# Moving weight-chunk loads behind the last unit's routing in an attention, FFN and top-1 MoE kernel

## Chip, cores and metric

One core of one Trainium2 chip. The metric is device microseconds (us) of one execution of the whole kernel, the median of several runs.

## What is computed

Three stages, all fp32, on 4 x 576 = 2304 tokens of width 512: sliding-window attention, a gated FFN and a top-1 mixture of 8 experts.

```python
def _moe_ref(x, w1, w2, w3, w_out):          # x: attention output, 2304 x 512
    return ((x @ w1) * (x @ w2) @ w3) @ w_out

def _moe2_ref(x, w_gate, w_output_gate, w1, w2):
    e_idx = np.argmax(x @ w_gate, axis=1)
    gate_w = softmax(x @ w_gate)[np.arange(N), e_idx]
    eom = sigmoid(x @ w_output_gate)
    for e in range(8):
        mask = e_idx == e
        ye = np.maximum(x[mask] @ w1[e], 0) @ w2[e]      # 512 -> 1024 -> 512
        out[mask] = gate_w[mask, None] * eom[mask, e, None] * ye
```

## The kernel before

Every fp32 product is three TensorE passes (`PASSES`) over operands split into a high part and a low part in the fp32r format: ScalarE (ACT) writes the high part, VectorE (DVE) subtracts it from the source to get the low part. An expert's two weight matrices are 4 MB; they come as 8 chunks of 512 KB. `items` numbers them: items 0 to 3 are w1 of expert 0, 4 to 7 its w2, 8 to 11 w1 of expert 1, 12 to 15 its w2, and so on. `eload` (line 658) issues a chunk's load on SyncE's queue (SP; line 666 for w1, 668 for w2) into one of three buffers (`ck2`, and a fourth, `ck3`, later); `esplit` is the split: `ehigh` on ACT (line 680), `elow` on DVE (line 684), which frees the buffer, and then a call of `eload` for what may be loaded next.

Attention and FFN run in 9 units of 256 tokens. Up to the end of the last unit's FFN a planner (`Plan`, a list scheduler) sets the order; `plan_end` gives it the first 11 chunk loads and 8 splits. TensorE (PE) follows the order of the program text; on the other engines the framework orders what is independent, and each engine then works through its list strictly in order.

Routing of the last unit (units before it are routed already): `x2_turn` and `logit` compute the logits `lg`; `_first` and `_onehot` the best expert as a one-hot `oh` on DVE; `_sum` is three small PE matmuls `rps` (lines 356 to 360) that count tokens per expert; `_rank` turns them into row numbers `pos` (line 376), `_gate` into the weights `ent` and the counts; two `_scatter`s on GpSimd (POOL, line 389) write 8-byte rows (token, weight) to `tab` in DRAM, sorted by expert. The 11 pieces are the list `post`, taken one by one by `step`.

Meanwhile PE works on the static block of expert 0 (`static_block`), 256 rows of `tab` that earlier units filled: for each of 8 feature blocks f, 12 matmuls `hps` (line 927), whose result becomes the high and low part of relu on ACT and DVE (lines 932, 933); then for each of two row blocks 24 matmuls `yps` with w2 (line 908), item 4 + f/2 being needed from f on. `at1` says after which (f, kk) of the hps part something is called, `at2` and `at3` after which f of the two yps parts; `step`s and `esplit`s are placed there. `rest` reads the rest of the rows: `rows` loads index rows from `tab` (line 705) and issues the gathers of token rows on POOL (line 711).

After the static block come the row turns for expert 0's remaining rows and expert 1's (`xT_block`: 4 transposes `gps`, line 732, then the high part `exT` on ACT, line 421, and the low part on DVE, line 422; two PSUM banks, so the third turn waits until the first is read), then expert 0's row block (`row_block`, matmuls `rps` of line 961), and then the static blocks of experts 1 to 7 with a row block each where an expert has more than 256 rows.

Of the kernel before, what the change touches and what calls it, by code (L numbers as in the profile page):

```python
# [9 lines left out]
F32 = mybir.dt.float32  # L10
# [3 lines left out]
I32 = mybir.dt.int32  # L14
# [7 lines left out]
NT, DM, DF, NE = B * S, H * D, 1024, 8  # L22
# [3 lines left out]
NTILE = NT // 128  # L26
# [370 lines left out]
def attention_moe_moe_kernel(ctx: ExitStack, tc: tile.TileContext, q0, k0, v, w1, w2, w3, w_out,  # L397
                             w_gate, w_ogate, ew1, ew2, out):
    nc = tc.nc
# [8 lines left out]
    tab = dram.tile([NE * NT, 2], I32, name="tab")  # L408
# [24 lines left out]
    rt = Router(tc, const, ps_ab, "ab", tab)  # L433
# [196 lines left out]
    exp_state = {}  # L630
    ex = [None]
# [23 lines left out]
    items = [(e, i, c) for e in range(NE) for i in range(2) for c in range(4)]  # L655
    nload, nsplit = [0], [0]

    def eload(to):
        while nload[0] < min(to, len(items)):
            e, i, c = items[nload[0]]  # L660
            if ex[0] is not None and nload[0] % 4 == 3:
                t = ex[0].tile([128, 1024], F32, name="ck3", tag="ck3", bufs=1)
            else:
                t = exp_state["p"].tile([128, 1024], F32, name="ck2", tag="ck2", bufs=3)
            if i == 0:
                nc.sync.dma_start(out=t, in_=ew1[e, 128 * c:128 * c + 128, :])
            else:
                nc.sync.dma_start(out=t.rearrange("p (a d) -> p a d", a=2),
                                  in_=ew2[e, 256 * c:256 * c + 256, :].rearrange("(a p) d -> p a d", p=128))
            eq.append(t)  # L670
            nload[0] += 1
# [7 lines left out]
    def ehigh():  # L679
        nc.scalar.activation(out=eparts()[0], in_=eq[0], func=AF.Copy)  # L680

    def elow(low=V):
        hi, lo = eparts()
        low.tensor_tensor(lo, eq.popleft(), hi.bitcast(F32), op=ALU.subtract)  # L684
        nsplit[0] += 1

    def esplit(low=V):
        if nsplit[0] < len(items):
            ehigh()
            elow(low)  # L690
            eload(nsplit[0] + (3 if ex[0] is None else 4))

    def step(n=1):
        for _ in range(n):
            if post:
                f, *a = post.popleft()
                f(*a)

    idx, xg, xTs = {}, {}, {}

    def rows(e, src, blocks, queue=None):

        n = src.shape[0] // 128
        t = idx[e] = exp_state["p"].tile([128, 4, 2], I32, name="idx", tag="idx", bufs=NE)
        (queue or nc.sync).dma_start(out=t[:, 0:n, :], in_=src.rearrange("(j p) x -> p j x", p=128))
        for j in range(blocks):
            gather(e, j)

    def gather(e, j):
        g = xg[e, j] = exp_state["p"].tile([128, DM], F32, name="xg", tag="xg", bufs=6)  # L710
        nc.gpsimd.indirect_dma_start(out=g, out_offset=None, in_=x2d[:, :],  # L711
                                     in_offset=bass.IndirectOffsetOnAxis(ap=idx[e][:, j, 0:1], axis=0))

    def early_rows(part):

        if part == 0:
            rt.count(256)
            t = idx["early"] = exp_state["p"].tile([128, 2, 2], I32, name="ixe", tag="ixe")
            nc.sync.dma_start(out=t, in_=tab[0:256, :].rearrange("(j p) x -> p j x", p=128))
            g = xg["early"] = moe.tile([128, 4, DM], F32, name="xt1", tag="xt1")  # L720
            nc.vector.memset(g[:, 0:2, :], 0.0)
        else:
            j = part - 1
            top = UNIT * (NU - 1)
            nc.gpsimd.indirect_dma_start(out=xg["early"][:, j, :], out_offset=None, in_=x2d[0:top, :],
                                         in_offset=bass.IndirectOffsetOnAxis(ap=idx["early"][:, j, 0:1], axis=0),
                                         bounds_check=top - 1, oob_is_err=False)
# [15 lines left out]
    def early_high(j):  # L743
        nc.scalar.activation(out=xTs[0][:, 0, :, 128 * j:128 * j + 128], in_=tps["e", j], func=AF.Copy)
# [108 lines left out]
    def plan_end():  # L853

        o = P.add("SP", 0.0, 0, open_exp, [done["x", n] for n in range(B * NP)], lat=0)
        for j in range(11):
            done["el", j] = P.add("DMA", 1.4, 400 + 5 * j, lambda j=j: eload(j + 1), [o], take=[("ck2", ("ck2", j))], lat=2.0)
        for j in range(8):

            k, c = divmod(j, 4)  # L860
            old = [done["gate", NU - 1, 2 * c + 1, k - 1]] if k else []
            h = P.add("ACT", 1.06, 400 + 5 + 5 * j, ehigh, [done["el", j]] + old + ([done["es", j - 1]] if j else []))
            done["es", j] = P.add("DVE", 1.22, 400 + 5 + 5 * j, elow, [h], give=[("ck2", j)])
        r = done["rows", NU - 2]
        r = P.add("DVE", 0.5, 400, lambda: early_rows(0), [r, o, done["free", 10], done["free", 11]], lat=4.0)
        for j in (1, 2):
            x = P.add("POOL", 1.1, 400, lambda j=j: early_rows(j), [r], lat=3.0)
            x = P.add("PE", 0.46, 400 + 55, lambda j=j: early_turn(j - 1), [x], take=[("S", ("early", j))])
            x = P.add("ACT", 0.6, 400 + 55, lambda j=j: early_high(j - 1), [x])
            P.add("DVE", 0.65, 400 + 55, lambda j=j: early_low(j - 1), [x], give=[("early", j)])  # L870
# [46 lines left out]
    def static_block(e, ix, at1, at2, at3, h_tile=h_tile, y_tile=y_tile):  # L917

        w1e = eslot(e, 0)
        xT = xTs.pop(e)  # L920
        hT = []
        for f in range(8):
            ps = (ps_v if f % 4 == 3 else ps_ab).tile([128, 512], F32, name="hps", tag="pv" if f % 4 == 3 else "ab")
            for kk in range(4):
                c = 1024 * kk + 128 * f
                for i, (a, b) in enumerate(PASSES):
                    mm(ps[:, 0:256], lhsT=w1e[a][:, c:c + 128], rhs=xT[:, b, kk, :],  # L927
                       start=kk == 0 and i == 0, stop=kk == 3 and i == 2)
                if (f, kk) in at1:
                    at1[f, kk]()  # L930
            h = h_tile(f)
            nc.scalar.activation(out=h[:, 0, :], in_=ps[:, 0:256], func=AF.Relu)
            nc.vector.scalar_tensor_tensor(out=h[:, 1, :], in0=ps[:, 0:256], scalar=0.0,
                                           in1=h[:, 0, :].bitcast(F32), op0=ALU.max, op1=ALU.subtract)
            hT.append(h)
            if f in at1:
                at1[f]()
        w2e = eslot(e, 1)
        for j, at in enumerate((at2, at3)):
            ps = mm2(hT, 128 * j, w2e, at)  # L940
            emit_out(ps, ix, j, y_tile)
# [52 lines left out]
    def rest():  # L994

        n0 = nc.values_load(rt.done[0:1, 0:1], min_val=0, max_val=256)
        rows(0, tab[bass.ds(n0, 128), :], 1, nc.scalar)
        rows(1, tab[NT:NT + 512, :], 3, nc.scalar)

    at1 = {k: lambda n=n: step(n) for k, n in {(0, 2): 1, (1, 0): 1, (1, 2): 1, (2, 0): 3, (3, 2): 3, (4, 1): 2}.items()}  # L1000
    at1.update({f: esplit for f in (5, 6, 7)})
    static_block(0, idx["early"], at1, {0: rest, 1: esplit, 4: esplit, 7: esplit}, {2: esplit, 5: esplit}, h_first, y_first)
    s_mo2.close()
    s_mo1.close()
    s_moe.close()
# [19 lines left out]
    n0 = nc.values_load(rt.done[0:1, 0:1], min_val=0, max_val=256)  # L1025
    n = nc.values_load(rt.cnt[0:1, 0:1], min_val=0, max_val=NT)
# [2 lines left out]
    begin(1)  # L1029
    turn()  # L1030
    gather(1, 3)
    with tc.If(n > n0):
        row_block(xT, idx[0], 0, w1e, w2e)
        with tc.If(n > n0 + 128):  # L1034
            row_loop(n0 + 128, n, w1e, w2e, xT)
    for e in range(1, NE):
        at1 = {f: esplit for f in (0, 2, 4, 6)}
        at1[1] = turn
        at3 = {3: esplit, 6: esplit}
        if e + 1 < NE:  # L1040
            rows(e + 1, tab[e * NT + NT:e * NT + NT + 512, :], 4)
            at3.update({0: lambda e=e: begin(e + 1), 2: turn, 5: turn})
        static_block(e, idx[e], at1, {f: esplit for f in (1, 5)}, at3)
        w1e, w2e = eslot(e, 0), eslot(e, 1)
        n = nc.values_load(rt.cnt[0:1, e:e + 1], min_val=0, max_val=NT)  # L1045
        with tc.If(n > 256):  # L1046
            xT = xTs.pop((e, 2))
            row_block(xT, idx[e], 2, w1e, w2e)
            with tc.If(n > 384):  # L1049
                xT_block(xg[e, 3], xT, 0)  # L1050
                row_block(xT, idx[e], 3, w1e, w2e)
                with tc.If(n > 512):  # L1052
                    row_loop(e * NT + 512, e * NT + n, w1e, w2e, xT)
# [49 lines left out]
```

## Time and profile before

| what | us |
|---|---|
| median of three runs | 787.07 (786.39 to 788.73) |
| profiled execution | 785.67 |
| its span | 784.0 |
| PE busy in the span | 734.4 |
| mean granted clock of PE | 0.985 of full |

The profiled execution is 1.40 us under the median. All times below are us from the start of its span. The stretch that the change touches runs from the last unit's FFN (about 488) to the start of expert 1's block (543.46): some 56 us. A timeline row gives the start, the length, the engine, the line, the operation and its tiles, the number of instructions drawn together, and in brackets the idle time before it with what ended it. SPq and ACTq are the queues on which SP and ACT issue DMAs.

### The profile page before, as it was taken

What the parts mean: (1) busy time and instruction counts of PE and PEld (TensorE: products, weight loads), DVE (VectorE), ACT (ScalarE), POOL (GpSimd) and SP (SyncE); (2) the same over time, 40 slices, a digit from 0 to 9 for tenths busy, and PEclk for the clock granted to TensorE, in tenths of its full rate; (3) what the DMA queues carried; (4) which work ended last, traced back from release to release, by engine and by line L of the source; (5) the groups of instructions that cost most, each with busy time, mean ns of one, the idle gap of its engine ahead of it and who ended that gap; (6) DMA issues with size and microseconds to landing.
All of it is one profiled execution on the core that took longest, in us unless ns stands there. A gap on an engine that the chain in (4) does not pass through costs nothing. (4 is left out here: it accounts for less than half of the span.)

```text
span 784.0 us, 13573 instructions
## 1 busy us (share of the span) xinstructions
PE 734.4 (94%) x5227; PEld 658.0 (84%) x5227; DVE 377.2 (48%) x907; ACT 302.0 (39%) x683; POOL 168.1 (21%) x196
## 2 busy tenths in 40 slices
PE   3799989999999999999999999879999999999995
PEld 2577778999999999999999998767888998988874
DVE  6987995543544444444324233813534661661110
ACT  2554443433333243344222123524445563553221
POOL 6554553110111311110020001123112212111010
PEclk9999998999999999999999999999999999999998
DMA  8946762421322222005000001783726772750010
GB/s 326 408 167 217 213 210 84 152 79 31 111 91 87 78 77 77 31 28 189 28 1 28 1 28 48 244 174 109 247 88 233 258 246 90 251 156 28 5 41 14
DMA packets 38934, 97.47 MB, mean 124 GB/s; under 512 B 9748, under 2 KB 9876, under 8 KB 38849
## 3 DMA queue, kind: packets, MB, share of 16 engines
q1 hardware_dynamic: 33072, 83.06, 32.0%
q0 software_dynamic: 4816, 12.77, 5.0%
q8 instruction: 50, 0.82, 0.5%
q10 hardware_dynamic: 960, 0.53, 0.2%
q14 instruction: 36, 0.29, 0.1%
HBM read 86.83 MB, written 10.65 MB: 124 GB/s over the span
## 5 line engine op out<-in xcount | busy, mean ns | idle before, releaser
L560 PE MATMUL ab<-xt,w 128*128 128x256 f32 x1728 | 229.2, 287 | 0.1
L560 PEld LDWEIGHTS ab<-xt,w 128*128 128x128 f32 x1728 | 219.1, 193 | 4.8 <-DVE f L513 0.3
L584 PE MATMUL acc<-w,gt 128*128 128x512 f32 x432 | 114.4, 399 | 3.4 <-ACT gt L572 2.6
L584 PEld LDWEIGHTS acc<-w,gt 128*128 128x128 f32 x432 | 76.1, 189 | 17.4 <-ACT gt L572 3.1
L568 DVE TENSOR_TENSOR a_sb<-ab,a_sb 128x256 f32<-128x256 f32 x72 | 30.5, 423 | 121.9 <-PE ab L560 113.5
L908 PE MATMUL yps<-w,hT 128*128 128x512 f32 x336 | 82.3, 395 | 0.0
L177 POOL TENSOR_TENSOR pp<-pp,r 128x384 f32<-128x384 f32 x48 | 39.6, 828 | 191.7 <-DVE r L172 160.5
L908 PEld LDWEIGHTS yps<-w,hT 128*128 128x128 f32 x336 | 61.3, 188 | 11.6
L572 ACT ACTIVATE gt<-a_sb 128x256 fp32r<-128x256 f32 x72 | 30.0, 416 | 100.3 <-DVE a_sb L568 95.6
L684 DVE TENSOR_TENSOR w<-ck,w 128x1024 fp32r<-128x1024 f32 x48 | 58.1, 1220 | 21.0 <-ACT w L680 14.4
L540 PE MATMUL wps<-w,w3T 128*128 128x512 f32 x192 | 52.7, 417 | 11.7 <-ACT w3T L527 11.6
L680 ACT ACTIVATE w<-ck 128x1024 fp32r<-128x1024 f32 x48 | 50.3, 1057 | 27.0 <-DMA ck<-in_moe_w 24.4
L900 POOL DMA_INDIRECT out<-y,idx x20 | 20.1, 1003 | 178.5 <-ACT y L899 124.1
L163 ACT ACTIVATE pp<-sps,nm 128x128 f32<-128x128 f32 x144 | 42.3, 368 | 39.4 <-DVE nm L154 37.2
L540 PEld LDWEIGHTS wps<-w,w3T 128*128 128x128 f32 x192 | 35.5, 196 | 19.4 <-ACT w3T L527 11.6
L927 PEld LDWEIGHTS hps<-exT,w 128*128 128x128 f32 x384 | 46.4, 192 | 3.5 <-issue 2.2
L927 PE MATMUL hps<-exT,w 128*128 128x256 f32 x384 | 47.4, 284 | 1.9 <-PEq L1049 0.9
L565 ACT ACTIVATE a_sb<-ab 128x256 f32<-128x256 f32 x72 | 27.8, 386 | 55.1 <-PE ab L560 51.9
L389 POOL DMA_INDIRECT tab<-ent,pos x18 | 17.6, 980 | 139.5 <-DVE pos L376 42.2
L422 DVE TENSOR_TENSOR exT<-gps,exT 128x512 fp32r<-128x512 f32 x23 | 15.9, 691 | 58.9 <-ACT exT L421 58.9
L576 DVE TENSOR_TENSOR gt<-a_sb,gt 128x256 fp32r<-128x256 f32 x72 | 31.3, 434 | 25.4 <-ACT gt L572 24.4
L145 PE MATMUL sps<-k,q 128*128 128x128 f32 x288 | 41.4, 282 | 1.0 <-DMA k<-in_k 1.0
(132 smaller groups left out, 1025.6 us busy)
## 6 DMA issues: line engine op xcount, KB each, us to landing
ck<-in_moe_w SPq DMA_DIRECT2D x88, 512.0 KB
q<-in_q SPq DMA_DIRECT2D x16, 576.0 KB
v<-in_v SPq DMA_DIRECT2D x16, 576.0 KB
k<-in_k SPq DMA_DIRECT2D x16, 320.0 KB
w<-in_moe_w_out SPq DMA_DIRECT2D x8, 512.0 KB
w<-in_moe_w SPq DMA_DIRECT2D x8, 512.0 KB
x2d<-x SPq DMA_DIRECT2D x16, 256.0 KB
x2d<-x ACTq DMA_DIRECT2D x2, 256.0 KB
```

Source lines behind the costliest of these rows:

```text
L145: nc.tensor.matmul(ps[:, 128 * i:128 * i + 128], lhsT=s["q"][:, 128 * c:128 * c + 128], rhs=s["k"][:, 64 * c:64 * c + 128], start=False, s ...
L163: nc.scalar.activation(out=p[:, o], in_=ps[:, o], func=AF.Exp, bias=nm[:, i:i + 1], scale=0.125)
L177: nc.gpsimd.tensor_tensor(p, p, s.pop(("r", g)).unsqueeze(2).to_broadcast([128, 3, 128]), op=ALU.mult)
L540: mm(ps, lhsT=t[:, a, 128 * j:128 * j + 128], rhs=wo[b][:, o:o + 512], start=g == 0 and j == 0 and x == 0, stop=g == 1 and j == 3 and x == 2)
L560: mm(ps, lhsT=w[a][:, c:c + 128], rhs=x[:, b, kk, :], start=kk == 0 and i == 0, stop=kk == 3 and i == 2)
L568: V.tensor_tensor(asb[u, m], gps.pop((u, m, 1)), asb[u, m], op=ALU.mult)
L576: V.tensor_tensor(g[:, 1, :], asb.pop((u, m)), g[:, 0, :].bitcast(F32), op=ALU.subtract)
L584: mm(accs[u][t], lhsT=g[:, a, 128 * t:128 * t + 128], rhs=ws["w34"][b][:, 512 * m:512 * m + 512], start=m == 0 and i == 0, stop=m == 7 and ...
L680: nc.scalar.activation(out=eparts()[0], in_=eq[0], func=AF.Copy)
L684: low.tensor_tensor(lo, eq.popleft(), hi.bitcast(F32), op=ALU.subtract)
L908: mm(ps, lhsT=hT[f][:, a, c0:c0 + 128], rhs=w[b][:, 512 * f:512 * f + 512], start=f == 0 and i == 0, stop=f == 7 and i == 2)
L927: mm(ps[:, 0:256], lhsT=w1e[a][:, c:c + 128], rhs=xT[:, b, kk, :], start=kk == 0 and i == 0, stop=kk == 3 and i == 2)
```

## The change

A chunk load can now be held back: `eload(to, behind)` first lets POOL copy one column of `behind` into the chunk's tile, and the load, which overwrites that tile, waits for the copy. The planner issues 6 loads and 6 splits instead of 11 and 8. Items 6 and 7 (the second half of expert 0's w2) are loaded behind `pos` (function `second`, called at (4, 3)) and split at f = 7. `rest` moves from the first yps part to f = 5 of the hps part, loads index rows 0 and 1 on SP's queue (ACT's before), and then loads items 8 to 10 behind `idx[1]`. `_sum`, `_rank` and `_gate` move from (3, 2) to (4, 0), which is 6 hps matmuls later, the scatters from (4, 1) to (4, 2). Splits and loads of items 8 and up come later: two in the second yps part, two before the row block, 9 instead of 8 in each of the blocks of experts 1 to 4. There are 4 buffers for index rows instead of 8, so the index loads of experts 4 to 7 wait for a buffer.

```diff
--- before.py
+++ after.py
@@ -655,13 +655,16 @@
     items = [(e, i, c) for e in range(NE) for i in range(2) for c in range(4)]
     nload, nsplit = [0], [0]
 
-    def eload(to):
+    def eload(to, behind=None):
+
         while nload[0] < min(to, len(items)):
             e, i, c = items[nload[0]]
             if ex[0] is not None and nload[0] % 4 == 3:
                 t = ex[0].tile([128, 1024], F32, name="ck3", tag="ck3", bufs=1)
             else:
                 t = exp_state["p"].tile([128, 1024], F32, name="ck2", tag="ck2", bufs=3)
+            if behind is not None:
+                nc.gpsimd.tensor_copy(t[:, 0:1], behind.bitcast(F32))
             if i == 0:
                 nc.sync.dma_start(out=t, in_=ew1[e, 128 * c:128 * c + 128, :])
             else:
@@ -688,7 +691,8 @@
         if nsplit[0] < len(items):
             ehigh()
             elow(low)
-            eload(nsplit[0] + (3 if ex[0] is None else 4))
+            if nsplit[0] > 8:
+                eload(nsplit[0] + (3 if ex[0] is None else 4))
 
     def step(n=1):
         for _ in range(n):
@@ -701,7 +705,7 @@
     def rows(e, src, blocks, queue=None):
 
         n = src.shape[0] // 128
-        t = idx[e] = exp_state["p"].tile([128, 4, 2], I32, name="idx", tag="idx", bufs=NE)
+        t = idx[e] = exp_state["p"].tile([128, 4, 2], I32, name="idx", tag="idx", bufs=4)
         (queue or nc.sync).dma_start(out=t[:, 0:n, :], in_=src.rearrange("(j p) x -> p j x", p=128))
         for j in range(blocks):
             gather(e, j)
@@ -853,9 +857,9 @@
     def plan_end():
 
         o = P.add("SP", 0.0, 0, open_exp, [done["x", n] for n in range(B * NP)], lat=0)
-        for j in range(11):
+        for j in range(6):
             done["el", j] = P.add("DMA", 1.4, 400 + 5 * j, lambda j=j: eload(j + 1), [o], take=[("ck2", ("ck2", j))], lat=2.0)
-        for j in range(8):
+        for j in range(6):
 
             k, c = divmod(j, 4)
             old = [done["gate", NU - 1, 2 * c + 1, k - 1]] if k else []
@@ -994,12 +998,21 @@
     def rest():
 
         n0 = nc.values_load(rt.done[0:1, 0:1], min_val=0, max_val=256)
-        rows(0, tab[bass.ds(n0, 128), :], 1, nc.scalar)
-        rows(1, tab[NT:NT + 512, :], 3, nc.scalar)
-
-    at1 = {k: lambda n=n: step(n) for k, n in {(0, 2): 1, (1, 0): 1, (1, 2): 1, (2, 0): 3, (3, 2): 3, (4, 1): 2}.items()}
-    at1.update({f: esplit for f in (5, 6, 7)})
-    static_block(0, idx["early"], at1, {0: rest, 1: esplit, 4: esplit, 7: esplit}, {2: esplit, 5: esplit}, h_first, y_first)
+        rows(0, tab[bass.ds(n0, 128), :], 1)
+        rows(1, tab[NT:NT + 512, :], 3)
+        eload(11, idx[1][:, 0, 0:1])
+
+    at1 = {k: lambda n=n: step(n) for k, n in {(0, 2): 1, (1, 0): 1, (1, 2): 1, (2, 0): 3, (4, 0): 3, (4, 2): 2}.items()}
+
+    def second():
+        eload(8, rt.pos[:, NTILE - 1:NTILE])
+
+    def both():
+        esplit()
+        esplit()
+
+    at1.update({(4, 3): second, 5: rest, 7: both})
+    static_block(0, idx["early"], at1, {}, {4: esplit, 7: esplit}, h_first, y_first)
     s_mo2.close()
     s_mo1.close()
     s_moe.close()
@@ -1029,6 +1042,8 @@
     begin(1)
     turn()
     gather(1, 3)
+    for _ in range(2):
+        esplit()
     with tc.If(n > n0):
         row_block(xT, idx[0], 0, w1e, w2e)
         with tc.If(n > n0 + 128):
@@ -1040,7 +1055,7 @@
         if e + 1 < NE:
             rows(e + 1, tab[e * NT + NT:e * NT + NT + 512, :], 4)
             at3.update({0: lambda e=e: begin(e + 1), 2: turn, 5: turn})
-        static_block(e, idx[e], at1, {f: esplit for f in (1, 5)}, at3)
+        static_block(e, idx[e], at1, {f: esplit for f in ((1, 3, 5) if e < 5 else (1, 5))}, at3)
         w1e, w2e = eslot(e, 0), eslot(e, 1)
         n = nc.values_load(rt.cnt[0:1, e:e + 1], min_val=0, max_val=NT)
         with tc.If(n > 256):
```

DVE, from the last logits of the routing to the one-hot `oh`. Before:

```order
L617 COPY lg<-lps 128x16
L684 TENSOR_TENSOR w_5832<-ck_5639,w_5831 128x1024
L338 TENSOR_REDUCE mx<-lg 128x2
L933 SCALAR_TENSOR_TENSOR xt_5691<-hps,xt_5691 128x256
L339 TENSOR_TENSOR d<-lg,mx 128x16
L684 TENSOR_TENSOR w_5832<-ck_5835,w_5831 128x1024
L341 SCALAR_TENSOR_TENSOR w<-d,wt 128x16
L381 TENSOR_REDUCE se<-ex 128x2
L343 TENSOR_REDUCE wm<-w 128x2
L383 TENSOR_SCALAR se<-se 128x2
L348 TENSOR_TENSOR oh<-w,wm 128x16
```

Of the change:

```order
L617 COPY lg<-lps 128x16
L338 TENSOR_REDUCE mx<-lg 128x2
L339 TENSOR_TENSOR d<-lg,mx 128x16
L341 SCALAR_TENSOR_TENSOR w<-d,wt 128x16
L343 TENSOR_REDUCE wm<-w 128x2
L381 TENSOR_REDUCE se<-ex 128x2
L348 TENSOR_TENSOR oh<-w,wm 128x16
```

The two splits (tile `ck`, 128x1024) and the relu part between the steps of the one-hot are gone from there.

ACT, from the end of the hps part of expert 0's static block to the high part of expert 0's rows (`exT` with a number). Before:

```order
L932 ACTIVATE xt_5813<-hps 128x256 [waits PE_49] x2
L680 ACTIVATE w_5921<-ck_5925 128x1024 [waits DMAHW6_49]
L932 ACTIVATE xt_5813<-hps 128x256 [waits PE_49]
L996 TENSOR_LOAD done [waits DVE_49]
L705 ISA
L705 DMA idx<-tab 128x2 [waits DMAHW1_49,DMASW3_49]
L705 DMA idx<-tab 128x4x2
L899 ACTIVATE xg<-yps,ixe 128x512 [waits PE_49] x2
L421 ACTIVATE exT_6017<-gps 128x512 [waits DMASW1_49,DMASW0_49,DMAHW7_49,DVE_49,PE_49]
```

Of the change (`ck_5799` and `ck_5802` are items 6 and 7; `ck_5849`, `ck_5852`, `ck_5855` items 8 to 10; `xg<-yps` is the block's result):

```order
L936 ACTIVATE xt_5805<-hps 128x256 [waits PE_49] x4
L683 ACTIVATE w_5306<-ck_5799 128x1024 [waits DVE_49,DMAHW5_49,Pool_49]
L683 ACTIVATE w_5306<-ck_5802 128x1024 [waits DMAHW6_49,Pool_49]
L903 ACTIVATE xg<-yps,ixe 128x512 [waits DMAHW2_49,PE_49]
L683 ACTIVATE w_5938<-ck_5849 128x1024 [waits DMAHW3_49,Pool_49]
L683 ACTIVATE w_5938<-ck_5852 128x1024 [waits DMAHW4_49,Pool_49]
L903 ACTIVATE xg<-yps,ixe 128x512 [waits PE_49]
L683 ACTIVATE w_5938<-ck_5855 128x1024 [waits DMAHW5_49,Pool_49]
L421 ACTIVATE exT_5996<-gps 128x512 [waits DMASW1_49,DMASW0_49,DMAHW1_49,DVE_49,PE_49]
```

Expert 0's `exT` now stands behind the splits of items 6 to 10; DVE's list has the low parts in the same order.

POOL, from the last unit's scatters on. Before:

```order
L389 DMA tab<-ent,pos 18432x2 [waits DMASW2_49,DVE_49]
L389 DMA tab<-ent,pos 18432x2 [waits DMASW3_49]
L711 DMA xg<-x2d,idx 128x512 [waits DVE_49,DMAHW7_49,DMAHW1_49,DMASW4_49]
L711 DMA xg<-x2d,idx 128x512 [waits DMAHW2_49,DMASW5_49]
L711 DMA xg<-x2d,idx 128x512 [waits DMASW6_49]
L711 DMA xg<-x2d,idx 128x512 [waits DMASW7_49]
L900 DMA out<-xg,ixe 2304x512 [waits DMASW0_49,Activation_49]
```

Of the change:

```order
L389 DMA tab<-ent,pos 18432x2 [waits DMASW2_49,DVE_49]
L389 DMA tab<-ent,pos 18432x2 [waits DMASW3_49]
L667 COPY ck_5799<-pos 128x1 [waits Activation_49]
L667 COPY ck_5802<-pos 128x1 [waits Activation_49]
L715 DMA xg<-x2d,idx 128x512 [waits DVE_49,DMAHW4_49,DMAHW7_49,DMAHW3_49,DMASW4_49]
L715 DMA xg<-x2d,idx 128x512 [waits DMAHW0_49,DMASW5_49]
L715 DMA xg<-x2d,idx 128x512 [waits DMASW6_49]
L715 DMA xg<-x2d,idx 128x512 [waits DMASW7_49]
L667 COPY ck_5849<-idx 128x1 [waits Activation_49]
L667 COPY ck_5852<-idx 128x1 [waits DMAHW5_49,DVE_49]
L667 COPY ck_5855<-idx 128x1 [waits DMAHW6_49,DVE_49]
L904 DMA out<-xg,ixe 2304x512 [waits DMASW0_49,Activation_49]
```

The copies that hold items 6 and 7 stand behind the scatters, those of items 8 to 10 behind the four gathers of index rows 0 and 1.

## Rows read from the trace of the kernel before

**Rows 1.** The page's first part: busy time of the engines, share of the span, instructions.
```profile
PE 734.4 (94%) x5227; PEld 658.0 (84%) x5227; DVE 377.2 (48%) x907; ACT 302.0 (39%) x683; POOL 168.1 (21%) x196
```
**Rows 2.** Timeline of PE from the last FFN matmuls to the first yps.
```profile
490.10 1.68 PE L584 MATMUL acc<-w,gt 128*128 128x512 f32 x6 [1.65 <-ACT gt L572]
...
496.01 1.07 PE L614 MATMUL lps<-gates,xt 128*128 128x16 f32 x8 [0.42 <-DVE xt L933]
...
503.11 0.17 PE L356 MATMUL rps<-oh,tri 128*128 128x16 bf16 x1 [2.18 <-DVE oh L348]
...
503.53 7.86 PE L927 MATMUL hps<-xt,wx 128*128 128x256 f32 x51
511.23 11.07 PE L908 MATMUL yps<-w,xt 128*128 128x512 f32 x48
```
**Rows 3.** Timeline of DVE in the last unit's routing.
```profile
499.64 0.16 DVE L617 COPY lg<-lps 128x16 f32<-128x16 f32 x1
499.72 1.21 DVE L684 TENSOR_TENSOR w<-ck,w 128x1024 fp32r<-128x1024 f32 x1
...
501.35 1.22 DVE L684 TENSOR_TENSOR w<-ck,w 128x1024 fp32r<-128x1024 f32 x1
...
502.89 0.17 DVE L348 TENSOR_TENSOR oh<-w,wm 128x16 bf16<-128x16 f32 x1
...
505.41 0.17 DVE L376 CAST pos<-pf 128x2 int32<-128x2 f32 x1
```
**Rows 4.** Windows: stretch, length, busy of five engines, then PEclk, DMA share, GB/s.
```profile
504.00:508.00 4.00, 4.00 (x24) 4.00 (x23) 2.91 (x11) 2.77 (x4) 1.77 (x2) 0.57 0.81 260
508.00:512.00 4.00, 4.00 (x33) 3.87 (x32) 3.15 (x5) 2.10 (x4) 0.21 (x1) 1.00 0.74 43
```
**Rows 5.** Timeline of SP's queue and ACT: two chunk loads, each with its first use.
```profile
487.02 0.38 SPq L668 DMA_DIRECT2D ck<-in_moe_w  x1
490.65 1.06 ACT L680 ACTIVATE w<-ck 128x1024 fp32r<-128x1024 f32 x1 [0.60 <-DMA ck<-in_moe_w]
493.00 0.33 SPq L666 DMA_DIRECT2D ck<-in_moe_w  x1
497.94 1.06 ACT L680 ACTIVATE w<-ck 128x1024 fp32r<-128x1024 f32 x1 [2.14 <-DMA ck<-in_moe_w]
```
**Rows 6.** Timeline, the group of tokens before: second scatter, index load, first gather.
```profile
467.79 0.96 POOL L389 DMA_INDIRECT tab<-ent,pos  x1 [0.30 <-issue]
471.03 0.39 SPq L719 DMA_DIRECT2D ixe<-tab  x1
476.12 1.04 POOL L725 DMA_INDIRECT xt<-x2d,ixe  x1 [7.38 <-issue]
```
**Rows 7.** Timeline, the last unit: second scatter, a chunk load, index load, two gathers.
```profile
507.25 0.96 POOL L389 DMA_INDIRECT tab<-ent,pos  x1 [0.30 <-issue]
508.68 0.34 SPq L666 DMA_DIRECT2D ck<-in_moe_w  x1
513.96 1.03 ACTq L705 DMA_DIRECT2D idx<-tab  x2
520.71 0.98 POOL L711 DMA_INDIRECT xg<-x2d,idx  x1 [12.50 <-issue]
522.55 0.96 POOL L711 DMA_INDIRECT xg<-x2d,idx  x1 [0.86 <-issue]
```
**Rows 8.** Timeline of PE from the last row turns to expert 1's block.
```profile
527.57 1.85 PE L732 MATMUL gps<-ident,xg 128*128 128x128 f32 x8 [2.90 <-DMA xg<-x2d,idx]
529.07 5.45 PE L961 MATMUL rps<-wx,exT 128*128 128x512 f32 x18
...
543.46 1.79 PE L927 MATMUL hps<-exT,w 128*128 128x256 f32 x13 [0.86 <-ACTq L1034]
```
**Rows 9.** Timeline of ACT and DVE: the two parts of expert 0's `exT`.
```profile
524.71 0.60 ACT L421 ACTIVATE exT<-gps 128x512 fp32r<-128x512 f32 x1 [1.69 <-PE gps L732]
525.34 0.69 DVE L422 TENSOR_TENSOR exT<-gps,exT 128x512 fp32r<-128x512 f32 x1 [12.43 <-ACT exT L421]
```

## The prediction

> **What bounds the kernel now.** I read the page's first part, then the timelines of PE, DVE, POOL and the queues between 488 and 545, then windows of that stretch for clock and DMA. PE is busy 734.4 of 784.0 us [rows 1], so only PE's gaps and stretches at the low clock can be won. Around the last unit's routing there are two kinds.
>
> First, before expert 0's yps part, PE waits 1.65 for an FFN gate, 0.42 for a relu part, and 2.18 for the one-hot `oh` [rows 2]. The last is DVE's queue: from the logits to `oh` 3.25 us pass, of which two chunk splits take 1.21 and 1.22 [rows 3]. Behind that wait the granted clock is 0.57 over 4 us [rows 4], that is 1.2 GHz for most of it, which costs 4 x 0.43 = 1.7.
>
> Second, behind the yps part (511.23 + 11.07 = 522.30) PE waits for token rows: the last two turns at 527.57 wait 2.90 for a gather, and the row block starts at 529.07 [rows 2, 8]. This second end has a chain of its own: scatter, index load, gather, transposes. What is won before 522.30 counts only as far as this chain moves too.
>
> **The change part by part.**
>
> *Splits out of the routing.* ACT's and DVE's lists have no chunk split left between the last FFN gate and `pos`. I count 0.9 of the 1.65 (one split of 1.06 or 1.22 no longer ahead of ACT and DVE, while the gate's own operations stay; ends 0 and 1.65), and all of 0.42 and 2.18: without the two splits the 3.25 is 0.8, and the ranks stand 6 hps matmuls later besides. 51 hps in 7.86 less the 1.7 of low clock is 0.12 each, so 0.7 for six. The rank matmuls start at 503.11 - 0.9 - 0.42 - 2.18 + 0.7 = 500.3; `oh` is due about 1.4 before that. From 503.11 to the yps part are 8.12; without the six matmuls (0.7) and the clock loss (1.7) 5.7 remain, so yps starts at 506.0 instead of 511.23: **5.2 won at this place**.
>
> *Items 6 and 7.* `pos` came 2.30 after the rank matmuls with a split of 1.2 in between [rows 2, 3]; now 1.1 to 1.5, so about 501.6. The second scatter was issued 1.84 after `pos` [rows 3, 7]: 503.4. POOL then makes two one-column copies. The trace has none on POOL; the smallest DVE operations take 0.16 [rows 3], the 128x512 part 0.69 [rows 9], and being tiny they are nearest the first: 0.2 each. The loads are issued at about 504.9 and 505.3. A load that finds the queue empty is in use 3.63 after its issue, one behind others 4.94 [rows 5]: they land at 508.5 and 510.2. With 1.06 and 1.22 for the parts of a split, item 6's low part is there at 510.8, item 7's at 512.5. A yps matmul takes 11.07 / 48 = 0.23, and the yps part wants these items from 506.0 + 12 x 0.23 = 508.8: it waits 2.0 and then 0.4. It ends at 506.0 + 11.07 + 2.4 = 519.5 instead of 522.30.
>
> *The index rows.* The two scatters and the two loads just behind them are the unclear place. In the group before, with nothing else on the DMA engines, it took 8.33 from the second scatter to the first gather (3.24 to the index load, 5.09 from there); in the last unit, with chunk loads all around, 13.46 (6.71 and 6.75) [rows 6, 7]. These are the two ends. I take 8.33, because now no chunk is in flight when the scatters are issued, as in the quiet group. The first gather is at 503.4 + 8.33 = 511.8, the second 1.84 later [rows 7], two more at 1.26 each (0.96 and a gap of 0.30 as between scatters): POOL is through at 517.4. That index rows 0 and 1 are now issued by SP and the index loads of experts 4 to 7 wait for buffers, I cost at nothing by itself: their users, blocks 2 to 7, come tens of us later.
>
> The Trainium skill (DMA: Bandwidth & Descriptors, "Queues, rings and completion order") says that SP and ACT each own one ring on every DMA engine, each worked through in order, and that an engine alternates between rings. It speaks against this part: index rows 0 would stand behind 1 MB of items 6 and 7, where ACT's ring could slip in between. In the trace the index load on ACT's queue, beside chunks on SP's, was no quick one (6.75 against 5.09), so the row doesn't bear the advantage out. By the rule the sum would have 6.75 for the second leg and end 1.7 higher.
>
> *Items 8 to 10, the new wait.* Their copies stand on POOL behind the four gathers, so their loads go out from 517.6 on, 0.4 apart. Landing is at 521.2 and then 1.31 apart (4.94 less 3.63): item 10 at 523.9. In the lists of ACT and DVE expert 0's `exT` stands behind item 10's split: high part of item 10 to 525.0, its low part to 526.2, then the low part of `exT` (0.69 [rows 9]) to 526.9. Before, `exT` was waiting for nothing but its transposes. The third row turn needs the bank that this frees, and stands in PE's list ahead of the row block; 4 transposes at the low clock are half of the 1.85 [rows 8], so the row block starts at **527.8 instead of 529.07: 1.3 won**. All else of the 5.2 and 2.8 is lost in this idle time of PE (520.4 to 526.9). Coming out of it PE runs at 1.2 GHz for some time: before, 18 row-block matmuls took 5.45 where 18 x 0.23 = 4.2 are the full clock's [rows 8, 2], and 1.5 lay between the first of those turns and the row block; now 0.9 lies there, so about 0.2 more of the block runs low. Net **-1.1**.
>
> *After it.* Row block to expert 1's block took 14.4 [rows 8]. It and all behind it stay: nine splits in a block instead of eight add 1.06 on ACT and 1.22 on DVE, engines that are 39% and 48% busy [rows 1]. If that cover were gone, a chunk would come up to one split (1.2) late in a block.
>
> **Sum.** -1.1 on the profiled 785.67 is 784.6; the median of the runs shown is 1.4 higher, so I predict 787.07 - 1.1 = **786.0**. 0.3%, or 2.4 us, is about what a measurement can tell from no change; this lies within. The bounds taken together: if the gate's 1.65 goes not at all, +0.9; if everything is at its good end, see the third rival.
>
> **Rivals.**
>
> 1. *The scatters and the loads behind them hamper each other: slower.* In the window from 508 to 512 the DMA engines were 0.74 busy and moved 43 GB/s, against 260 in the window before [rows 4], though a chunk load had been issued at 508.68, 1.43 behind the second scatter, and another soon after [rows 7]. The scatter itself counted as landed only 6.71 after its issue. Items 6 and 7 are now issued 1.5 behind the second scatter, in the same position. If the chain takes 13.46 again, the first gather, items 8 to 10, `exT` and the row block come 5.1 later: -1.1 + 5.1 = +4.0, 791.1. The yps part's longer wait for item 6 is hidden in that. It is slower than the measurement's bound from a chain of 11.9 on. For it: same distance, same kinds of transfer, and no other place of the trace has a chunk load so close behind a scatter. Against it: before, the scatters came into a stream of chunks, now into an empty queue. The Trainium skill (same page, "Specifications") says that transfers under 512 B are read-modify-write, as these 8-byte rows would be; no row shows whether that is what slows the loads.
> 2. *Index rows behind the chunks on one queue.* If the index load waits on SP's queue until items 6 and 7 are in, its leg is as long as the loaded one: 3.24 and 6.75 are 9.99 instead of 8.33, +1.7, that is 787.6. For it: two 512 KB loads are issued just before the index loads; against it: 5.09 from 506.7 ends at 511.8, and by then both chunks have landed.
> 3. *Everything at its good end: faster.* `pos` 0.3 sooner, gathers 1.26 apart from the first (0.6), item 10 in use 4.94 after its issue at 518.4, 0.6 sooner, and no low clock added (0.2): -1.1 - 1.7 = -2.8, 784.3. For it: the DMA queues carry little else then. Against it: it takes all of them.
> 4. *Chunks late in the blocks of experts 1 to 4.* They now run up to four chunks behind before, with fewer loaded ahead; one wait of 0.5 to 1.2 per block is +2 to +4, less the 1.1: 788 to 790. Against it: ACT and DVE have room.
>
> That the change doesn't do what it says has no place here: POOL works in order, so the copies do come behind the scatters and gathers.
>
> **How the numbers follow.** Forecast 0.42, first rival 0.24, second 0.10, third 0.17, fourth 0.07. The range runs from 783.6, the third rival less 0.7 (the lowest of the three runs is that much under their median), to 790.8, nearly all of the first rival; the forecast alone is good for 784.4 to 787.6. Faster: the third rival, and the forecast's lower edge, 0.24. Slower: the first, half of the fourth and a little for partial hampering, 0.31. Same: the rest, 0.45.
>
> **What would show it.** The wait for `oh` and the low clock behind it gone; yps starting near 506 and standing about 2.4 in its middle for items 6 and 7; the first gather 8 to 10 us behind the second scatter; the third row turn of PE waiting some 6 us, ended by `exT` on DVE; the row block near 527.8. The prediction is wrong if the chain from scatter to gather takes over 11.9, if `exT` isn't what ends PE's wait, or if new waits show up in the blocks from 543 on.

## Result and profile after

The change makes the kernel slower: 797.95 us (median of five) against 786.39, ratio 1.014 with a 95% interval from 1.0119 to 1.0162, some 11 us. The forecast was 786.0, the range 783.6 to 790.8. One of the five, the one profiled with the result, took 2541 us with every matmul about three times as long; the ratio leaves it out (the other four have a median of 797.60), and the lines here are of a further execution of the same kernel: 797.58, span 795.9, against 784.0 before.

PE's timeline, page row and rows of the second half, to be read against [rows 1, 2, 8]:

```profile
PE 733.6 (92%) x5227; PEld 656.2 (82%) x5227; DVE 378.6 (48%) x907; ACT 301.9 (38%) x683; POOL 171.4 (22%) x201
```

```profile
487.20 1.95 PE L584 MATMUL acc<-w,gt 128*128 128x512 f32 x6 [0.55 <-ACT gt L572]
...
498.02 0.18 PE L356 MATMUL rps<-oh,tri 128*128 128x16 bf16 x1
...
503.53 2.91 PE L912 MATMUL yps<-w,xt 128*128 128x512 f32 x12
513.82 0.79 PE L912 MATMUL yps<-w,xt 128*128 128x512 f32 x1 [7.38 <-ACT w L683]
515.08 10.03 PE L912 MATMUL yps<-w,xt 128*128 128x512 f32 x35 [0.47 <-DVE w L687]
...
533.30 1.12 PE L736 MATMUL gps<-ident,xg 128*128 128x128 f32 x4 [7.32 <-DVE exT L422]
534.07 5.33 PE L965 MATMUL rps<-wx,exT 128*128 128x512 f32 x18
...
548.00 3.12 PE L931 MATMUL hps<-exT,w 128*128 128x256 f32 x24 [0.86 <-ACTq L1049]
...
621.36 2.93 PE L931 MATMUL hps<-exT,w 128*128 128x256 f32 x12 [2.00 <-DVE hT L937]
650.25 1.69 PE L931 MATMUL hps<-exT,wx 128*128 128x256 f32 x12 [3.04 <-DVE hT L937]
676.60 11.77 PE L931 MATMUL hps<-exT,w 128*128 128x256 f32 x96 [0.43 <-PEq L1064]
```

The work is the same (733.6 busy, 734.4 before), so the loss is waiting. The routing's waits are gone: from the last FFN matmuls to yps it takes 503.53 - 487.20 = 16.3, where it was 21.1 [rows 2]. Then come four new waits: 7.38 for item 6, 7.32 for `exT`, and 2.00 and 3.04 in the blocks of experts 3 and 4. Expert 1's block begins at 548.00 instead of 543.46 (+4.5). This execution was 1.8 us ahead already at the FFN matmuls of 226.21 (228.01 before), long before anything that the change touches; counted from there, the loss up to expert 1's block is 6.3. From expert 1's block to expert 5's it takes 676.60 - 548.00 = 128.6; before, that stretch was this:

```profile
543.46 3.12 PE L927 MATMUL hps<-exT,w 128*128 128x256 f32 x24 [0.86 <-ACTq L1034]
...
664.95 11.78 PE L927 MATMUL hps<-exT,w 128*128 128x256 f32 x96 [0.43 <-PEq L1049]
```

That is 121.5, so in this execution **7.1 of the 11.9** are lost in the blocks of experts 1 to 4, and 0.3 behind them.

The same execution on POOL, SP's queue, ACT and DVE, against [rows 5, 6, 7, 9]:

```profile
501.01 0.96 POOL L389 DMA_INDIRECT tab<-ent,pos  x1 [0.31 <-issue]
501.97 0.31 POOL L667 COPY ck<-pos 128x1 f32<-128x1 f32 x2
502.19 0.90 SPq L671 DMA_DIRECT2D ck<-in_moe_w  x2
508.50 2.63 SPq L709 DMA_DIRECT2D idx<-tab  x4
512.71 1.06 ACT L683 ACTIVATE w<-ck 128x1024 fp32r<-128x1024 f32 x1 [8.60 <-DMA ck<-in_moe_w]
515.09 1.00 POOL L715 DMA_INDIRECT xg<-x2d,idx  x1 [12.81 <-DMA idx<-tab]
...
519.86 0.42 POOL L667 COPY ck<-idx 128x1 f32<-128x1 f32 x3
520.08 1.29 SPq L669 DMA_DIRECT2D ck<-in_moe_w  x3
527.03 1.06 ACT L683 ACTIVATE w<-ck 128x1024 fp32r<-128x1024 f32 x1 [6.65 <-DMA ck<-in_moe_w]
...
532.56 1.28 DVE L422 TENSOR_TENSOR exT<-gps,exT 128x512 fp32r<-128x512 f32 x2
```

From the second scatter to the first gather 14.1 us pass, not 8.33. This chain has two legs: 7.5 to the issue of the index load, and 6.6 from there to the gather. Item 6 is in use 10.5 after its load's issue, item 8 6.95, both 3.63 in the forecast. The windows (columns as in [rows 4]) show the DMA engines occupied but moving little behind the scatters (0.40 busy at 32 GB/s from 504 to 510), and the low granted clock around and behind PE's wait (0.50, that is 1.2 GHz, from 510 to 518):

```profile
500.00:504.00 4.00, 4.00 (x35) 3.91 (x34) 1.14 (x3) 1.04 (x3) 1.97 (x4) 1.00 0.01 1
504.00:510.00 6.00, 2.43 (x11) 1.69 (x9) 0.42 (x1) 0.11 (x1) 0.00 (x0) 0.89 0.40 32
510.00:518.00 8.00, 3.72 (x8) 2.63 (x9) 2.45 (x2) 2.11 (x2) 2.30 (x3) 0.50 0.50 144
```

### The profile page after: what moved, and what is told of

The parts are those of the page before. It is cut to its first block, busy times and chain, and to the rows that moved or that the text cites. A ratio compares the mean times of both kernels' runs of the same rounds, so it can differ in the third digit from the quotient of the medians.

```text
span 2539.3 us, 13593 instructions
## 1 busy us (share of the span) xinstructions
PE 2511.9 (99%) x5227; PEld 1914.5 (75%) x5227; DVE 387.0 (15%) x907; ACT 309.3 (12%) x683; POOL 171.1 (7%) x201
## 4 chain that ended last, share of the span: by engine, by line
PE 66%; issue 31%; DMA 1%; POOL 1%; DVE 0%; ACT 0%; POOLq 0%; another core or an unknown queue 0%; SPq 0%; ACTq 0%; DVEq 0%
PE ab L560 28%; PE acc L584 14%; PE wps L540 6%; PE sps L145 5%; PE tps L184 2%; PE pv L201 2%; PE lps L614 2%; PE hps L931 2%; PE yps L912 2%; DMA out<-y,idx 1%; PE xps L603 1%; PE sps L141 1%; POOL xg L715 1%; PE pvt L201 0%; POOL out L904 0%
## 5 line engine op out<-in xcount | busy, mean ns | idle before, releaser
L560 PEld LDWEIGHTS ab<-xt,w 128*128 128x128 f32 x1728 | 721.3, 537 | 46.5 <-issue 41.4
L560 PE MATMUL ab<-xt,w 128*128 128x256 f32 x1728 | 748.1, 679 | 0.0
L584 PE MATMUL acc<-w,gt 128*128 128x512 f32 x432 | 379.7, 1108 | 1.0 <-ACT gt L572 1.0
L912 PE MATMUL yps<-w,hT 128*128 128x512 f32 x336 | 287.2, 1105 | 0.0
L584 PEld LDWEIGHTS acc<-w,gt 128*128 128x128 f32 x432 | 190.9, 468 | 107.2 <-issue 97.2
L540 PE MATMUL wps<-w,w3T 128*128 128x512 f32 x192 | 168.8, 1123 | 11.5 <-ACT w3T L527 11.5
L145 PEld LDWEIGHTS sps<-k,q 128*128 128x128 f32 x288 | 120.7, 455 | 15.8 <-issue 9.6
L912 PE MATMUL yps<-w,h 128*128 128x512 f32 x144 | 123.4, 1109 | 0.0
L931 PEld LDWEIGHTS hps<-exT,wx 128*128 128x128 f32 x288 | 118.0, 601 | 5.3 <-issue 5.3
L931 PE MATMUL hps<-exT,wx 128*128 128x256 f32 x288 | 119.5, 670 | 0.7 <-PEq L1064 0.4
```

Of the source, the lines that this page charges most:

```text
L145: nc.tensor.matmul(ps[:, 128 * i:128 * i + 128], lhsT=s["q"][:, 128 * c:128 * c + 128], rhs=s["k"][:, 64 * c:64 * c + 128], start=False, s ...
L540: mm(ps, lhsT=t[:, a, 128 * j:128 * j + 128], rhs=wo[b][:, o:o + 512], start=g == 0 and j == 0 and x == 0, stop=g == 1 and j == 3 and x == 2)
L560: mm(ps, lhsT=w[a][:, c:c + 128], rhs=x[:, b, kk, :], start=kk == 0 and i == 0, stop=kk == 3 and i == 2)
L584: mm(accs[u][t], lhsT=g[:, a, 128 * t:128 * t + 128], rhs=ws["w34"][b][:, 512 * m:512 * m + 512], start=m == 0 and i == 0, stop=m == 7 and ...
L912: mm(ps, lhsT=hT[f][:, a, c0:c0 + 128], rhs=w[b][:, 512 * f:512 * f + 512], start=f == 0 and i == 0, stop=f == 7 and i == 2)
```

## Experiments

Theories: **A**, chunk loads close behind the scatters and the scatter's chain hamper each other (the first rival); **B**, `exT` behind the splits of items 8 to 10 makes the wait before the row block; **C**, chunks come late in the blocks of experts 1 to 4 (the fourth rival). The kernel before, run beside them, had medians of 785.35 (first group), 785.13 (second) and 786.1 (the last kernel). Diffs are against the changed kernel.

**The change once more.** No edit.

> The changed kernel once more, for a profile in which TensorE runs as usual (in the one that came with the result every matmul took about three times as long, 2540 us). Theory A (chunk loads issued 1.2 us behind the second scatter hamper the chain scatter, index load, gather): 13 to 14 us from the second scatter to the first gather, as before the change, and the row block of expert 0 about 5 us later than forecast (533 instead of 527.8). Theory B (expert 0's exT behind the splits of items 8 to 10): TensorE's wait before the row block is ended by exT on VectorE and lasts over 8 us. Theory C (chunks late in the blocks of experts 1 to 4): further waits for weight splits after expert 1's block begins. A and B together make +4 to +5 of the +11 measured; what is left is C's or the low clock's. Time 797 to 798.

796.07, ratio 1.0123 (1.009 to 1.0155). All three show, in the lines above: A with 14.1, B with 7.32 ended by `exT` on DVE, C with the 7.1.

**Items 6 and 7 not held.**

```diff
-        eload(8, rt.pos[:, NTILE - 1:NTILE])
+        eload(8)
```

> The copies that hold items 6 and 7 behind the ranks are left out; these loads go as soon as a buffer is free, well ahead of the scatters. Items 8 to 10 stay held behind the index rows. Theory A: 8.3 to 10 us from the second scatter to the first gather, everything behind it 4 to 5 us earlier, about 793. If A is wrong (the chain is slow whatever is issued near it): 13 to 14 us again and within 1.5 us of the changed kernel, since the yps part's wait is hidden behind the gathers. Theory B and C keep the rest, +5 to +7 over the kernel before.

792.14, ratio 1.0088 (1.006 to 1.0116), 3.9 less than the change by the medians, though the intervals overlap. The timeline of POOL, SP's queue and PE:

```profile
503.27 0.96 POOL L389 DMA_INDIRECT tab<-ent,pos  x1 [0.31 <-issue]
509.49 1.95 SPq L709 DMA_DIRECT2D idx<-tab  x4
512.82 0.98 POOL L715 DMA_INDIRECT xg<-x2d,idx  x1 [8.59 <-DMA idx<-tab]
517.80 9.29 SPq L669 DMA_DIRECT2D ck<-in_moe_w  x4
530.56 1.11 PE L736 MATMUL gps<-ident,xg 128*128 128x128 f32 x4 [12.31 <-DVE exT L422]
```

The chain is 9.55, as A expects, and yps runs through without a wait. But PE now waits 12.31 for `exT`: the yps part's wait had been hidden behind this one, so only what the chain gains gets through. Counted from the last FFN matmuls (488.46 here), the row block comes 42.9 later instead of 46.9. Of the chain's 4.5, 3.3 are won in the second leg (3.3 instead of 6.6) and 1.3 in the first, which stays at 6.2 though no chunk is near.

**Items 8 to 10 not held.**

```diff
-        eload(11, idx[1][:, 0, 0:1])
+        eload(11)
```

> The copies that hold items 8 to 10 behind index rows 1 are left out, those of items 6 and 7 stay. Their loads then stand on SP's queue right behind the index loads and go as buffers come free. Theory A alone: chain of 13 to 14 us stays, and the loads no longer wait for the gathers, so exT is no longer late: 4 to 6 us faster than the changed kernel, about 792 to 794. Theory B: the same, and TensorE's wait before the row block is ended by a gather, not by exT. Theory C: still waits in the blocks behind, time within 2 us of the changed kernel.

792.38, ratio 1.0074 (1.0046 to 1.0102), as expected in time. The chain is 13.8 (503.60 to 517.44), and PE's wait before the row block falls to 4.20. It is still `exT` that ends it, not a gather: that part of the expectation was wrong, the loads come late enough by themselves.

```profile
532.87 1.12 PE L736 MATMUL gps<-ident,xg 128*128 128x128 f32 x4 [4.20 <-DVE exT L422]
```

**No load held** (both edits).

> No copy holds any load; the moved steps, the later splits, four index buffers and index loads on SP stay. Theories A and B: nearly all of the loss goes, 786 to 789, with 8.3 to 10 us (A, if no load stands close behind the scatters) or 13 (if loads of items 8 and on do) from the second scatter to the first gather. Theory C: the later splits stay, so 790 or more, with waits for weights in the blocks of experts 1 to 4.

788.94, ratio 1.0045 (1.0027 to 1.0062). Expert 1's block starts at 542.40, 1.1 ahead of the kernel before, but the blocks of experts 1 to 4 take 124.1 (121.5), with waits of 1.58 and 0.75 for relu low parts: C is there without any held load. The chain is 11.4 here, between A's two values. One thing was not as expected: the splits are not late in this kernel. PE waits 1.98 for `oh` again.

**Eight index tiles.**

```diff
-        t = idx[e] = exp_state["p"].tile([128, 4, 2], I32, name="idx", tag="idx", bufs=4)
+        t = idx[e] = exp_state["p"].tile([128, 4, 2], I32, name="idx", tag="idx", bufs=NE)
```

> The change with eight index tiles, as before; all else of it stays. Theory C1 (with four tiles an index load waits in SP's queue for the output scatter that used its tile, and the chunk loads behind it come 4 us late, in the blocks of experts 3 and 4): the PE waits for relu low parts of 2.0 and 3.0 in those blocks go, with the low clock behind them, so 6 to 7 us faster than the change, 789 to 790. Theory C2 (nine splits in a block are too many, or chunks are late because fewer were loaded ahead): at most 1 us faster, 795 or more, the waits stay.

790.12, ratio 1.007 (1.0046 to 1.0094): 5 over the kernel before instead of 11. The blocks of experts 1 to 4 take 122.2 (547.14 to 669.29). Over all the runs here it is the same: with four index tiles this stretch took 124.0 to 128.6 in seven profiles, with eight 121.4 to 122.6 in four. The reason stands in expert 3's block of the change (POOL, SP's queue, ACT):

```profile
609.91 1.00 POOL L904 DMA_INDIRECT out<-y,idx  x1 [1.17 <-ACTq L1061]
613.88 0.38 SPq L709 DMA_DIRECT2D idx<-tab  x1
614.35 2.63 SPq L671 DMA_DIRECT2D ck<-in_moe_w  x4
618.66 1.06 ACT L683 ACTIVATE w<-ck 128x1024 fp32r<-128x1024 f32 x1 [4.14 <-DMA ck<-in_moe_w]
```

and with eight tiles:

```profile
611.86 4.80 SPq L671 DMA_DIRECT2D ck<-in_moe_w  x4
615.83 1.06 ACT L683 ACTIVATE w<-ck 128x1024 fp32r<-128x1024 f32 x1 [1.60 <-DMA ck<-in_moe_w]
```

The index load waits until the output scatter of 609.91 has landed (its tile is that scatter's list of rows), and four chunk loads stand behind it on SP's queue. ACT waits 4.14 for the first instead of 1.60, its split holds up the relu parts behind it in the lists of ACT and DVE, and these hold up PE (the 2.00 of the result).

**Eight splits in a block instead of nine.**

```diff
-        static_block(e, idx[e], at1, {f: esplit for f in ((1, 3, 5) if e < 5 else (1, 5))}, at3)
+        static_block(e, idx[e], at1, {f: esplit for f in (1, 5)}, at3)
```

> The change with eight splits per block as before instead of nine (two in the first yps part), four index tiles stay. C1: the waits in the blocks of experts 3 and 4 stay, within 2 us of the change, 794 to 798; one split fewer behind a late chunk may save some. C2 by the number of splits: the waits go, 789 to 790.

794.19, ratio 1.0127 (1.0101 to 1.0152), no different from the change's 1.0123. The waits stay, at 1.50 and 0.60 here. That is smaller than the 2.00 and 3.04 of the change, but other runs with nine splits have waits of this size too (1.58 and 0.75 with no load held), so a part of the ninth split isn't shown. The index tiles are the cause.

**No load held, eight index tiles.**

> No copy holds a load, and eight index tiles: what is left of the change are the moved steps, later splits and index loads on SP. By C1 it loses the 2.6 that the run without copies still lost in the blocks of experts 1 to 4 and keeps the 1.0 that expert 1's block began earlier: 784 to 785, about 1 below the kernel before. If C1 is wrong, 788 to 789 again.

783.91, ratio 0.999 (0.9974 to 1.0005): level with the kernel before. The blocks of experts 1 to 4 take 121.4, without these waits. So the whole loss goes with the copies and the four tiles. But the run doesn't show what later splits are worth, because here, as in the run with no load held, they are not late:

```profile
502.22 0.17 PE L356 MATMUL rps<-oh,tri 128*128 128x16 bf16 x1 [1.92 <-DVE oh L348]
```

With the copies gone and the loads early, the framework has put chunk splits back between the logits and the one-hot (on DVE at 498.46 and 500.24, the places of [rows 3]), though the program text calls them later. In the change it was the held loads that kept the splits out of the routing.

**Without the scatters**, and **items 6 and 7 behind index rows 0**, to see what holds the loads up:

```diff
-    post.extend(rt.parts(*GROUPS[NU - 1]))
+    post.extend(rt.parts(*GROUPS[NU - 1])[:-2])
```

> The change without the last unit's two scatters, so that the table lacks the rows of the last 256 tokens and their outputs are left out; the loads of items 6 and 7 are still held behind the ranks. Theory A1 (the scatters' 8-byte writes hold up reads that follow within a few us): item 6 is in use 3.6 to 5 us after its load is issued, as elsewhere, instead of 10.5, and yps waits 0 to 2.5 instead of 7.4. Theory A2 (something else at that place holds the loads up: the copy that gates them, or a fetch of code): 8 to 11 us again and a wait of 5 to 8.

```diff
         rows(0, tab[bass.ds(n0, 128), :], 1)
+        eload(8, idx[0][:, 0, 0:1])
...
-    at1.update({(4, 3): second, 5: rest, 7: both})
+    at1.update({5: rest, 7: both})
```

> The change with items 6 and 7 held behind index rows 0 instead of the ranks, so that their loads go out some 10 us after the second scatter instead of 1.2. Theory A1: their loads take 3.6 to 5 us from issue to use, and the scatter's chain to the first gather is 9 to 10 us instead of 14; yps still waits some 9 us, now because the loads go out late. Theory A2 (copy): 8 to 11 us from issue to use here too, and a wait of 14.

One execution each, 785.9 and 796.47 beside 786.96 of the kernel before; the first leaves work out, so only its waits are read. Load and first use of item 6, without scatters:

```profile
499.32 0.89 SPq L671 DMA_DIRECT2D ck<-in_moe_w  x2
503.06 1.06 ACT L683 ACTIVATE w<-ck 128x1024 fp32r<-128x1024 f32 x1 [0.98 <-DMA ck<-in_moe_w]
```

and behind index rows 0, 11 us after the second scatter:

```profile
501.35 0.97 POOL L389 DMA_INDIRECT tab<-ent,pos  x1 [0.31 <-issue]
511.34 0.98 POOL L715 DMA_INDIRECT xg<-x2d,idx  x1 [9.03 <-DMA idx<-tab]
512.55 0.88 SPq L671 DMA_DIRECT2D ck<-in_moe_w  x2
517.08 1.06 ACT L683 ACTIVATE w<-ck 128x1024 fp32r<-128x1024 f32 x1 [12.63 <-DMA ck<-in_moe_w]
```

3.7 and 4.5 us instead of 10.5, with a copy in front of the load in both. A fetch of code, the other half of A2, is out too: from 501 to 510 the DMA queues of the change carried only packets of the scatters and of the chunks. So it is the scatters, and only for a few us behind them. The chain behaves as A1 expects, 10.0 with the loads behind it, while yps waits 11.42 for the late loads. Over all the runs it took 13.0 to 14.1 in the four profiles at the usual speed with two loads 1.2 us behind the second scatter, and 9.5 to 10.0 in the four with no load near. Without the scatters the load of item 8 still takes 6.9 to first use (510.80 to 517.74): it stands behind the gathers and just ahead of the first output scatter, and gains nothing from the missing scatters. Which of these two holds it up was not tried.

**Row turns first.** Items 6 and 7 not held, eight tiles, items 8 to 10 held behind index rows 0, and ACT and DVE in the order of the text from the turns on:

```diff
-    xT_block(xg[0, 0], xT, 0)
-    begin(1)
-    turn()
-    gather(1, 3)
-    for _ in range(2):
-        esplit()
-    with tc.If(n > n0):
+    with tc.manual_schedule(engines={E.Activation, E.DVE}):
+        xT_block(xg[0, 0], xT, 0)
+        begin(1)
+        turn()
+        gather(1, 3)
+        for _ in range(4):
+            esplit()
+        with tc.If(n > n0):
...
```

> A try at a version that is faster than both: items 6 and 7 not held, eight index tiles, items 8 to 10 held behind index rows 0 (their copies ahead of the last three gathers), and on ACT and DVE the row turns ahead of the splits of items 8 to 11, all of these ahead of the row block. Theory B (exT's place behind these splits makes the wait before the row block): the third turn is no longer ended by exT late, the row block starts at 520 to 524 instead of 529 (before) and 534 (change), and expert 1's block at 536 to 540, 777 to 782. If the gathers themselves are slowed by the three loads beside them, the row block stays at 527 to 530, 784 to 788.

780.98, ratio 0.9951 (0.9934 to 0.9969), faster than both. The row block starts at 522.87, expert 1's block at 537.05.

**The same with no load held**: the copies go too, and items 8 to 10 are requested right behind the splits of 6 and 7.

> No load is held: items 6 to 10 are loaded as buffers come free, well before the scatters, and only split late (on ACT and DVE the row turns stand ahead of the splits of items 8 to 11, these ahead of the row block; eight index tiles). By A1 and B together no chunk is in flight beside scatters, index rows or gathers and exT waits for no chunk: 9 to 10 us from the second scatter to the first gather, the row block at 519 to 521 instead of 523 in the version before it, expert 1's block at 533 to 536, 776 to 779. If holding the loads back mattered beyond that, or the gathers are slow by themselves, no better than 781.

**778.36, ratio 0.9902 (0.9879 to 0.9926), 1% below the kernel before.** Timeline of SP's queue, POOL and PE:

```profile
488.18 5.11 SPq L669 DMA_DIRECT2D ck<-in_moe_w  x3
503.75 0.97 POOL L389 DMA_INDIRECT tab<-ent,pos  x1 [0.31 <-issue]
513.62 0.98 POOL L715 DMA_INDIRECT xg<-x2d,idx  x1 [8.90 <-DMA idx<-tab]
520.55 0.69 PE L736 MATMUL gps<-ident,xg 128*128 128x128 f32 x4 [1.27 <-DMA xg<-x2d,idx]
521.15 5.87 PE L965 MATMUL rps<-wx,exT 128*128 128x512 f32 x18
535.64 3.12 PE L931 MATMUL hps<-exT,w 128*128 128x256 f32 x24 [0.86 <-ACTq L1050]
```

Items 8 to 10 are loaded 10 us ahead of the scatters and split behind the turns; the chain is 9.9, and the third turn waits 1.27 for its gather instead of 7.32 for `exT`. There is no wait for `oh`: here the fixed order of ACT and DVE from the turns on keeps the splits of items 8 to 11 out of the routing, where the run above without copies had let them back in.

## Why the prediction was wrong

*Splits out of the routing: right.* From the FFN matmuls to yps I had 506.0 - 489.2 = 16.8; it is 16.3. The wait for `oh` and the low clock behind it are gone (1.00 from 500 to 504). What did it was the held loads, as the runs without copies show.

*The index tiles: the step that failed most.* "I cost at nothing by itself: their users, blocks 2 to 7, come tens of us later." The users do come late, but the index load doesn't wait alone: what is queued behind it on SP are the next chunks. I had asked who waits for the index rows and not what stands behind their load. The price is 6.4 in two profiles (128.6 and 122.2 for the blocks of experts 1 to 4) and 5.7 in the medians (10.7 over the kernel before, 5.0 with eight tiles); in the other six profiles with four tiles the blocks took 124.0 to 126.5, so the 128.6 is a high one. My fourth rival had late chunks in these blocks, but from fewer loads ahead, and at 0.5 to 1.2 each; the waits are 2.00 and 3.04, and behind the first the granted clock is lower (0.86 from 621 to 633).

*From scatter to gather: the wrong end.* I took 8.33, "because now no chunk is in flight when the scatters are issued". None was, but two are issued 1.2 us behind, and the chain took 14.1: the first rival, at its upper price of 13.46. The run without scatters shows a direction that I had left open: the scatters slow the loads. The loads then lengthen mostly the second leg (by 3.3 of 4.5), where the index rows stand behind them on one queue, the place of my second rival. What part the queue has in that was not separated. And 8.33 was out of reach in any case: in the four runs with no load near, the legs are 6.2 to 6.7 and 3.1 to 3.5, where I had 3.24 and 5.09; that these sums are only 1.2 to 1.7 above 8.33 is luck. The Trainium skill (DMA: Bandwidth & Descriptors, "Specifications") has transfers under 512 B as read-modify-write. No run here shows whether that is how the scatters slow the loads.

*Items 6 and 7:* 7.38 and 0.47 instead of 2.4, from the same cause. As the first rival said, this wait is hidden for the most part: yps ended at about 525, and `exT` came 8 us later still.

*Items 8 to 10: right in kind, too small.* The third row turn waited 7.32, ended by `exT` on DVE, where I had 6.5. But I took 3.63 for a load that finds the queue empty, while four gathers had just been issued and an output scatter followed: item 8 took 6.95, and item 10 started its split 10.3 after the first of these loads (530.34), not 6.3. From the FFN matmuls to the row block it was 46.9 instead of my 38.6: 5.8 from the chain and 4.0 from these loads, less about 1.5 by which scatter, POOL and splits were quicker than I had put them.

*Index rows on SP's queue.* The second leg was 6.6 with items 6 and 7 ahead in the same queue and 3.3 without them (the first experiment). From ACT's queue, with chunks on SP's, it had been 6.75 [rows 7], so a queue of its own was no cure there. The Trainium skill (DMA: Bandwidth & Descriptors, "Queues, rings and completion order") has each engine's ring worked through in order. The 6.6 and the 3.3 agree with that; no run here tried the index rows of the change on ACT's queue.

## What to carry to other kernels

Before a buffer count is lowered, list what stands behind the transfer that will wait for the buffer on its in-order queue; the transfer's own user may be far away and the loss still be several us. A large load that is issued right behind scatters of small rows is better sent well ahead of them: holding it back until "after" put it into the worst place. And holding a load also moves its consumers: in the lists of ACT and DVE everything behind a late split is late, so it is the split that should be moved behind urgent work, not the load. A later call in the program text isn't enough for that where a framework orders the list: look at the order that comes out.

## What the runs showed that I had not expected

Two scatters of 128 rows of 8 bytes, 1 KB each, cost a 512 KB load issued 1.2 us behind them nearly 7 us (10.5 from issue to use against 3.7 without the scatters and 4.5 when sent 11 us behind them). In the stretch of low throughput the DMA engines count as 0.40 busy at 32 GB/s.

The leg from the second scatter to the index load is 6.2 in the first experiment, where no chunk is near, against 3.24 in the group of tokens before [rows 6]. In its window from 503 to 509 the DMA queues carried only the scatters and two fetches of code:

```profile
q8 instruction: 1, 0.02, 3.5%
q14 instruction: 1, 0.01, 2.0%
q0 software_dynamic: 64, 0.00, 0.9%
```

The last column is the share of 16 engines' time in 6 us: one fetch of 16 KB took 3.5% of 96, 3.4 us, and one of 8 KB 1.9. In the run without scatters an 8 KB fetch took 0.45 (1.4% of 32 from 503 to 505). The chain's first leg doesn't need both to be long: it was 6.5 in the run behind index rows 0, with no 16 KB fetch in it, and 6.7 in the last kernel, whose 8 KB fetch took 0.5. And the group before, which I had called quiet, had a 16 KB fetch as well, of 2.4 us (1.9% of 128, counted at 471), with a first leg of 3.24. Whether such fetches hold the scatter's landing up, or are only slowed by it as the chunks are, stays open.
